# Chunk-selected attention into a soft mixture of experts on one core: the order of five groups of steps

## The chip, the core and the metric
The kernel runs on one core of a Trainium2 chip. The core has a matrix engine (TensorE, PE in the profile, with its weight loads listed as PEld), a vector engine (VectorE, DVE), a scalar engine (ScalarE, ACT), a general engine (GpSimd, POOL) and a queue engine (SyncE, SP). Each takes its own instructions strictly in order; between engines, semaphores make one wait for another. Matrix products are written to PSUM, everything else lies in SBUF. The metric is device time in microseconds (us); every difference below is in us too.

## The reference
Four batches of eight heads, 768 positions, 64 numbers per head. Keys are cut into 24 chunks of 32. Per query, an upper bound of its score with each chunk is worked out from the chunk's smallest and largest key; the six chunks with the highest bounds are kept, and attention runs over those, causally:

```python
k_min = np.min(k_chunks, axis=3)
k_max = np.max(k_chunks, axis=3)
ub = np.sum(np.maximum(q * k_min, q * k_max), axis=-1)      # per query and chunk
ub = np.where(causal, ub, -1e9)
top_chunks = np.argsort(ub, axis=-1)[..., -6:]
scores = np.where(selected & causal_by_position, scale * q @ k.T, -1e9)
x = softmax(scores) @ v                                      # 3072 rows of 512
logits = x @ phi                                             # 32 slots: 8 experts of 4
slot_input = softmax(logits, axis=0).T @ x                   # over all 3072 rows
slot_out = relu(slot_input @ w1[e]) @ w2[e]                  # per expert, 512 -> 1024 -> 512
out = softmax(logits, axis=1) @ slot_out
```

## The kernel before
The heads are worked in 16 pairs, four pairs to a batch. The order of the work is written out by hand: the loop over pairs `i` (from line 618) issues steps of several pairs in turn, and each engine runs its share in just that order. Tiles in PSUM come from three small pools: `sc` (two tiles, scores), `at` (one tile, the attention output) and `tp` (two tiles, everything else: transposes, bounds, logits). A step that takes a tile of `tp` has to wait until the tile two before it has been read.

In turn `i` the steps are, by function and engine:

- `scores(i, g)` for six groups `g`: PE forms scores (L323) and adds a large negative number for chunks not selected (L333); `expo(i, g)`: ACT's exponential into `e_sb` (L347), then POOL zeroes what lies above the diagonal (L357).
- `ubound(i + 1)`: PE's bounds for the next pair, into `ub_ps` (L275, L282), from `qpn` and `bd`.
- `normalise(i - 2)`: DVE's reciprocal and product into `x_sb` (L387, L388), which empties the only `at` tile.
- `select(i + 1)`: DVE finds the largest bounds (`mx`, L294) and marks what falls below the sixth (`ns_t`, L297).
- `transposes(i + 2, "k")`, `evac_T`: PE transposes k into `tr_ps` (L231), ACT copies it to `kT` (L240); the same for q later in the turn.
- `pv(i - 1, ...)`: PE multiplies `e_sb` with v into `at_ps` (L375), in parts spread over the turn; the first part has to find `at` empty.
- `x_transposes(i - 2)`, `evac_x`: PE and DVE transpose `x_sb` (L397, L408).
- `kmin`, `kmax` (i + 2): DVE's smallest and largest keys, `mm` (L249, L255); `kmax` also forms `bd`, one block per head (L257).
- `ns_transposes(i + 1)`, `evac_ns`: PE transposes the marks (L305), DVE copies them to `nsT` (L313), which the next turn's scores need.
- `qsplit(i + 2)`: DVE's negative and positive parts of q, `qpn` (L265, L269).

When the last pair of a batch is through attention, that batch's MoE steps join the turns (`moe(step, i)` acts only on the last pair of a batch). At the end of turns 5, 9 and 13 come the logits (L420) and, on DVE, `pm` and a copy of the logits (L429, L430). Turns 6, 10 and 14 then hold `pmT` (PE, L436), `mb` (DVE, L443), the exponentials of both softmaxes (ACT into `d_sb`, L470, and into `c_pad`, L494 to L498), `moe_dispatch` (PE into `si_ps`, L509; DVE adds to `si_acc`, L516 to L527) and `moe_ct`: PE transposes the combine weights `c_pad` into `cT_ps` (L532) and DVE copies them to `cT_all` (L540).

Behind the loop, the last batch's MoE steps run alone. The experts follow: hidden layer into `h_ps` (L834), ACT's rectification into `h_sb` (L841), transposes into `hT_ps` (L846) and DVE's copy into `hT_pad` (L850), in two halves `f` of the hidden layer. The second layer accumulates in `so_ps`: `experts_out(f)` for experts 0 to 3 (L873), each in a quarter of the rows, `shared_out()` for experts 5 to 7 (L889), whose 24 products are dealt out over the four quarters so that four run beside each other, and `last_expert_out` for expert 4, in two halves of the columns (L899), whose weights are the last to be loaded. `slot_sums` (L854) gives the softmax's sums. `so_part` (L931) and `so_all` (L933, L935) scale the result, and the last products with `cT_all` give the output, which SP's queue writes.

All loads are issued from POOL's queue, in the order in which the steps stand there: q and k five pairs ahead, v two pairs ahead (L162), and the experts' weights one or two to a turn (`load_w`, L145). The weights of the last expert are issued at the start of turn 15.

Of the kernel before, what the change touches and what calls it, by code (L numbers as in the profile page):

```python
# [59 lines left out]
def kernel(  # L60
# [21 lines left out]
    LAST = NPAIR - 1  # L82
# [8 lines left out]
    st = {}  # L91
# [126 lines left out]
    def warm(n):  # L218
        r = ones_sq.rearrange("p (o c) -> p o c", o=1).broadcast_to([P, 4, P])
        for _ in range(n):  # L220
            for x in range(2):
                nc.tensor.matmul(
                    warm_ps[:, 2 * x:2 * x + 2], lhsT=ones_sq, rhs=r[:, :2], start=True, stop=True)

    def transposes(i, nm):

        ps = p_tp.tile([P, NQT, P], BF16, name="tr_ps", tag="tp")
        src = st.pop((nm, i))
        for g in range(NQT):
            for h in range(2):  # L230
                nc.tensor.matmul(  # L231
                    ps[h * 64:(h + 1) * 64, g, :], lhsT=src[:, h, g * D:(g + 1) * D], rhs=ident,
                    is_transpose=True,
                )
        st[nm + "ps", i] = ps

    def evac_T(i, nm):

        t = tp3.tile([P, S], BF16, name=nm + "T", tag=nm + "T")
        nc.scalar.copy(  # L240
            t.rearrange("d (p g) -> d p g", g=NQT),
            st.pop((nm + "ps", i)).rearrange("d g p -> d p g"),
        )
        st[nm + "T", i] = t
# [7 lines left out]
    def kmax(i):  # L252
        kT = st["kT", i].rearrange("d (c x) -> d c x", x=CH)
        mm = st.pop(("mm", i))
        nc.vector.tensor_reduce(mm[:, 1, 0, :], kT, axis=AX.X, op=ALU.max)  # L255
        bd = tpu.tile([P, 2, 2, NCHUNK], BF16, name="bd", tag="bd")
        nc.vector.tensor_tensor(  # L257
            bd, mm.broadcast_to([P, 2, 2, NCHUNK]), headsel.broadcast_to([P, 2, 2, NCHUNK]), op=ALU.mult,
        )
        st["bd", i] = bd  # L260

    def qsplit(i):
        qT = st["qT", i]
        t = tpu.tile([P, 2, S], BF16, name="qpn", tag="qpn")
        nc.vector.tensor_scalar_min(t[:, 0, :], qT, 0.0)  # L265
        if i == 0:
            nc.scalar.activation(t[:, 1, :], qT, func=ACT.Relu)
        else:
            nc.vector.tensor_scalar_max(t[:, 1, :], qT, 0.0)  # L269
        st["qpn", i] = t  # L270
# [40 lines left out]
    def evac_ns(i):  # L311
        t = tp2.tile([P, NJ * P], BF16, name="nsT", tag="nsT")
        nc.vector.tensor_copy(t, st.pop(("nsps", i)).rearrange("p t c -> p (t c)"))  # L313
        st["nsT", i] = t
# [25 lines left out]
    def expo(i, g, masked=True):  # L340
        pieces = (GROUPS_LAST if i == LAST else GROUPS)[g]
        w = sum(x[2] for x in pieces)
        if w == 512:
            e = ep.tile([P, 2, 512], BF16, name="e_sb", tag="e_sb")
        else:
            e = ep3.tile([P, 2, 384], BF16, name="e3_sb", tag="e3_sb")
        nc.scalar.activation(e[:, :, :w], st.pop(("scps", i, g))[:, :, :w], func=ACT.Exp, scale=scale)  # L347

        st["e", i, g] = e
        if masked:  # L350
            mask(i, g)
# [191 lines left out]
    def have(i):  # L543
        return 0 <= i < NPAIR

    def moe(step, i):

        if have(i) and i % NPB == NPB - 1:
            step(i // NPB)
# [5 lines left out]
    def weights(i):  # L555
        nonlocal nw
        for _ in range(wplan.get(i, 0)):
            load_w(nw)
            nw += 1
# [3 lines left out]
    evac_T(0, "k")  # L563
    kmin(0)
    kmax(0)
    warm(2)
    transposes(0, "q")
    evac_T(0, "q")
# [15 lines left out]
    evac_ns(0)  # L584
    kmin(1)
    kmax(1)
    qsplit(1)
    nc.gpsimd.dma_start(out=phi_sb, in_=moe_phi.rearrange("(hg p) s -> p hg s", p=P))
    nc.gpsimd.affine_select(
# [23 lines left out]
    kmin(2)  # L613
    evac_ns(1)
    kmax(2)
    qsplit(2)

    for i in range(1, NPAIR):
        slots = have(i - 3) and (i - 3) % NPB == NPB - 1
        if i >= EARLY:  # L620
            wt = ctx.enter_context(tc.tile_pool(name=f"wt{i}", bufs=1))
            w_sb.append(wt.tile([P, NFG * Dm], BF16, name=f"w_sb{i}"))
            weights(i)
        if have(i + 5) and not slots:
            load(i + 5, "k")
            load(i + 5, "q")
        scores(i, 0)
        expo(i, 0)
        moe(moe_max, i - 3)
        scores(i, 1)  # L630
        expo(i, 1)
        if have(i + 1):
            ubound(i + 1)
        moe(moe_bound, i - 3)
        if have(i - 2):
            normalise(i - 2)
        if i == LAST:
            moe_ct_copy(B - 2)
        if have(i + 1):
            select(i + 1)  # L640
        moe(moe_comb, i - 3)
        if have(i + 2):
            transposes(i + 2, "k")
            evac_T(i + 2, "k")
        if not slots:
            if have(i + 2):
                load_v(i + 2)
            if i < EARLY:
                weights(i)
        pv(i - 1, [0, 1, 2])  # L650
        for g in (2, 3):
            scores(i, g)
            expo(i, g, not slots)
        moe(moe_exp, i - 3)
        if slots:
            mask(i, 2)
            mask(i, 3)
        if have(i + 5) and slots:
            load(i + 5, "k")
            load(i + 5, "q")  # L660
        if have(i - 2):
            x_transposes(i - 2)
        pv(i - 1, [3] if i < LAST else [3, 4])
        if have(i + 2):
            transposes(i + 2, "q")
            evac_T(i + 2, "q")
            kmin(i + 2)
        moe(moe_exp2, i - 3)
        if have(i - 2):
            evac_x(i - 2)  # L670
        if have(i + 2):
            kmax(i + 2)
        moe(moe_scale, i - 3)
        if slots:
            if have(i + 2):
                load_v(i + 2)
            if i < EARLY:
                weights(i)
        scores(i, 4)
        expo(i, 4)  # L680
        if i == LAST:
            pv(i - 1, [5])
        moe(moe_comb2, i - 3)
        scores(i, 5)
        expo(i, 5)
        if have(i + 1):
            ns_transposes(i + 1)
            evac_ns(i + 1)
        if i < LAST:
            pv(i - 1, [4])  # L690
        moe(moe_dispatch, i - 3)
        if i < LAST:
            pv(i - 1, [5])
        if have(i + 2):
            qsplit(i + 2)
        moe(moe_ct, i - 3)
        moe(moe_logits, i - 2)
        moe(moe_copy, i - 2)
        if i == LAST - 2:
            l_ctx.close()  # L700
        if i == LAST - 1:
            u_ctx.close()
# [140 lines left out]
    def hidden_T(f):  # L843
        hT_ps = p_tp.tile([P, 4, P], BF16, name="hT_ps", tag="tp")
        for x in range(4):
            nc.tensor.matmul(hT_ps[:, x, :], lhsT=h_sb[:, f, x::4], rhs=ident, is_transpose=True)  # L846
        for g in range(2):
            o = hT_pad[:, f * 4:(f + 1) * 4, g * 4:(g + 1) * 4, g * SPE:(g + 1) * SPE]
            i_ = hT_ps.rearrange("p a (j s) -> p a j s", j=4)[:, :, :, g * SPE:(g + 1) * SPE]
            nc.vector.tensor_copy(o, i_)  # L850
# [19 lines left out]
    def experts_out(f):  # L870
        for fg in range(f * 4, (f + 1) * 4):
            for e in range(4):
                nc.tensor.matmul(  # L873
                    so_ps[e * CH:(e + 1) * CH, :], lhsT=hT_pad[:, fg, e, :],
                    rhs=w_sb[E + e][:, fg * Dm:(fg + 1) * Dm], start=(fg == 0), stop=False,
                )

    def shared_out():
        parts = [
            [(5, x) for x in range(6)],  # L880
            [(5, 6), (5, 7), (6, 0), (6, 1), (6, 2), (6, 3)],
            [(6, 4), (6, 5), (6, 6), (6, 7), (7, 0), (7, 1)],
            [(7, x) for x in range(2, 8)],
        ]
        for n in range(6):
            for j in range(4):
                e, fg = parts[j][n]
                c0 = e * CH - (SPE if j == e - 5 else 0)
                nc.tensor.matmul(  # L889
                    so_ps[j * CH:(j + 1) * CH, :], lhsT=hT[:, fg, c0:c0 + CH],  # L890
                    rhs=w_sb[E + LATE.index(e)][:, fg * Dm:(fg + 1) * Dm], start=False, stop=(n == 5),
                )
# [31 lines left out]
    w_ctx.close()  # L924
    op = ctx.enter_context(tc.tile_pool(name="op", bufs=5))
    experts_out(0)
    hidden_T(1)
    slot_sums()
    experts_out(1)
    shared_out()  # L930
    nc.vector.tensor_scalar_mul(so_part, so_ps[:, HD:], zinv)  # L931
    last_expert_out(1)
    nc.vector.scalar_tensor_tensor(so_sb[1], so_last, zinv, so_part, op0=ALU.mult, op1=ALU.add)  # L933
# [17 lines left out]
    n = 0  # L951
# [44 lines left out]
```

## Time and profile before

| | |
|---|---|
| median of 3 runs | 161.38 us (161.33 to 162.57) |
| the profiled execution | 161.03 us, span 159.3 us |
| busy PE, DVE, ACT, POOL | 137.7, 122.7, 122.1, 103.0 us |
| chain that ended last, by engine | PE 48%, ACT 17%, DVE 12%, DMA 8% |
| loop over pairs, from the first exponential to the last | about 12.8 to 124.8 us |
| experts' layers | 131.0 to 140.1 us |
| output | 140.1 us to the end |

Busy time is how long an engine had an instruction running. Products on PE overlap each other and their ends are modelled, so a busy PE can still have room. The chain follows the last instruction back, at each step to what released it. In the timelines below, a number in brackets is how long the engine sat idle before the row, and behind the arrow stands what it waited for. "issue" there means that the profile names no other engine.

### The profile page before, as it was taken

Reading aid. Unit: us, or ns where it says so; the run is one execution under the profiler, and the core shown is the slowest. Engines: PE = TensorE matmul, PEld = TensorE weight load, DVE = VectorE, ACT = ScalarE, POOL = GpSimd, SP = SyncE. Lnnn points to the kernel's source line nnn. Section 1 sums busy time; section 2 is a strip of 40 time slices with the busy share of each in tenths; the row PEclk is TensorE's granted clock in tenths of the full one; section 3 lists DMA queues with packets and bytes.
Section 4 is the critical chain, followed back from the end, with each engine's and each line's share of the span. In section 5 each row is a group of like instructions: output and inputs, shape, how many; then the busy total and the mean of one; then the engine's idle time right before and its main releaser. Section 6 shows DMA issues by size and latency. Waiting matters only on the chain.

```text
span 159.3 us, 5926 instructions
## 1 busy us (share of the span) xinstructions
PE 137.7 (86%) x2435; PEld 93.6 (59%) x2436; DVE 122.7 (77%) x436; ACT 122.1 (77%) x168; POOL 103.0 (65%) x201
## 2 busy tenths in 40 slices
PE   7796779999999998999999989999898999978400
PEld 5473446767667776767777766767667854433000
DVE  5367889999999998999999699999952751287620
ACT  3288879999999898999989889998788632076510
POOL 6979779599797679888766976759574710000000
PEclk9999999999999999999999999999999999999965
DMA  2999999999999999999999999999999999239996
GB/s 39 149 179 202 190 208 206 185 203 205 182 208 198 202 207 200 204 183 207 198 203 203 202 203 204 201 207 194 210 203 214 215 214 200 60 116 406 406 402 251
DMA packets 40571, 32.92 MB, mean 207 GB/s; under 512 B 26336, under 2 KB 34784, under 8 KB 40544
## 3 DMA queue, kind: packets, MB, share of 16 engines
q0 software_dynamic: 38384, 26.25, 110.6%
q1 hardware_dynamic: 2160, 6.29, 10.1%
q8 instruction: 19, 0.31, 0.7%
q14 instruction: 8, 0.07, 0.1%
HBM read 52.49 MB, written 6.29 MB: 369 GB/s over the span
## 4 chain that ended last, share of the span: by engine, by line
PE 48%; ACT 17%; DVE 12%; DMA 8%; issue 6%; POOL 4%; DVEq 0%; ACTq 0%; SPq 0%; POOLq 0%
ACT e_sb L347 11%; PE sc_ps L323 9%; PE at_ps L375 8%; PE sc_ps L333 6%; DMA out_dram<-o_sb 5%; PE tr_ps L231 5%; PE xT_ps L397 4%; ACT qT L240 4%; DMA q_in<-in_q_dram 3%; DVE x_sb L388 3%; PE h_ps L834 2%; PE ub_ps L282 2%; PE ub_ps L275 1%; DVE mx L294 1%; PE so_ps L873 1%
## 5 line engine op out<-in xcount | busy, mean ns | idle before, releaser
L347 ACT ACTIVATE e_sb<-sc_ps 128x1024 bf16<-128x1024 f32 (+1 forms) x96 | 83.1, 917 | 6.6 <-PE sc_ps L333 6.0
L357 POOL TENSOR_SCALAR_AFFINE_SELECT e_sb<-e_sb 128x256 bf16<-128x256 bf16 x96 | 39.8, 437 | 12.0 <-ACT e_sb L347 11.6
L323 PE MATMUL sc_ps<-qT,kT 64*128 64x384 bf16 (+3 forms) x258 | 36.8, 306 | 2.6 <-ACT e_sb L347 1.7
L333 PE MATMUL sc_ps<-nsT,smask 64*128 64x384 bf16 (+2 forms) x294 | 38.1, 284 | 0.1
L375 PE MATMUL at_ps<-v_t,e_sb 128*128 128x65 bf16 x642 | 28.4, 194 | 1.6 <-DVE x_sb L388 1.4
L375 PEld LDWEIGHTS <-e_sb 128*128 128x128 bf16 x642 | 24.5, 98 | 3.8 <-issue 2.5
L323 PEld LDWEIGHTS <-kT 64*128 64x128 bf16 x258 | 13.9, 93 | 10.7 <-issue 5.3
L294 DVE MAX8 mx<-ub_ps 128x8 f32<-128x8 f32 (+1 forms) x192 | 16.8, 162 | 4.0 <-PE ub_ps L282 3.8
L162 POOL DMA_DIRECT2D v_t<-in_v_dram x16 | 16.6, 1040 | 3.4 <-PE xT_ps L397 1.4
L249 DVE TENSOR_REDUCE mm<-kT 128x24 bf16<-128x768 bf16 x16 | 15.1, 943 | 3.1 <-ACT kT L240 3.1
L333 PEld LDWEIGHTS <-smask 64*128 64x128 bf16 x294 | 15.0, 94 | 3.8 <-issue 0.6
L240 ACT COPY kT<-tr_ps 128x768 bf16<-128x768 bf16 x16 | 12.9, 804 | 4.3 <-PE tr_ps L231 4.3
L388 DVE TENSOR_TENSOR x_sb<-at_ps,inv 128x768 bf16<-128x768 f32 (+1 forms) x17 | 15.5, 910 | 0.6
L255 DVE TENSOR_REDUCE mm<-kT 128x24 bf16<-128x768 bf16 x16 | 15.1, 943 | 0.0
L240 ACT COPY qT<-tr_ps 128x768 bf16<-128x768 bf16 x16 | 12.8, 799 | 2.8 <-PE tr_ps L231 2.8
L145 POOL DMA_DIRECT2D w_sb<-in_moe_w_dram x16 | 11.4, 714 | 1.5 <-DMA w_sb<-in_moe_w_dram 1.5
L152 POOL DMA_DIRECT2D k_in<-in_k_dram x14 | 10.2, 726 | 3.0 <-PE tr_ps L231 1.6
L152 POOL DMA_DIRECT2D q_in<-in_q_dram x14 | 10.1, 720 | 0.5 <-PE sc_ps L333 0.3
L408 DVE COPY xT_sb<-xT_ps 128x768 bf16<-128x768 bf16 (+1 forms) x15 | 8.0, 537 | 2.5 <-PE xT_ps L397 2.5
L231 PE MATMUL tr_ps<-ident,q_in 128*64 128x128 bf16 x192 | 8.4, 223 | 1.1 <-DMA q_in<-in_q_dram 0.8
L231 PE MATMUL tr_ps<-ident,k_in 128*64 128x128 bf16 x192 | 8.7, 229 | 0.2
L397 PE MATMUL xT_ps<-ident,x_sb 128*128 128x128 bf16 x96 | 8.3, 221 | 0.3 <-DVE x_sb L388 0.3
(147 smaller groups left out, 209.0 us busy)
## 6 DMA issues: line engine op xcount, KB each, us to landing
w_sb<-in_moe_w_dram POOLq DMA_DIRECT2D x16, 1024.0 KB, 15.5
out_dram<-o_sb SPq DMA_DIRECT2D x10, 512.0 KB, 4.6
v_t<-in_v_dram POOLq DMA_DIRECT2D x16, 192.0 KB, 11.6
k_in<-in_k_dram POOLq DMA_DIRECT2D x14, 192.0 KB, 10.6
q_in<-in_q_dram POOLq DMA_DIRECT2D x14, 192.0 KB, 10.9
out_dram<-o_sb SPq DMA_DIRECT2D x2, 256.0 KB, 4.1
k_in<-in_k_dram POOLq DMA_DIRECT2D x1, 384.0 KB, 7.3
q_in<-in_q_dram POOLq DMA_DIRECT2D x1, 384.0 KB, 8.4
```

The costliest lines, as they stand in the source:

```text
L152: nc.gpsimd.dma_start(out=t, in_=src.rearrange("h (p g) d -> p h (g d)", p=P))
L162: nc.gpsimd.dma_start(out=v_t[i % NV][:, :, :, :D], in_=v[b, 2 * j:2 * j + 2].rearrange("h (g p) d -> p h g d", p=P),)
L231: nc.tensor.matmul(ps[h * 64:(h + 1) * 64, g, :], lhsT=src[:, h, g * D:(g + 1) * D], rhs=ident, is_transpose=True,)
L240: nc.scalar.copy(t.rearrange("d (p g) -> d p g", g=NQT), st.pop((nm + "ps", i)).rearrange("d g p -> d p g"),)
L249: nc.vector.tensor_reduce(mm[:, 0, 0, :], kT, axis=AX.X, op=ALU.min)
L294: nc.vector.max(mx[:, a, :], ub[:, a, :max(8, 4 * t + 4)])
L323: nc.tensor.matmul(ps[:, h, c:c + w], lhsT=kT[r, kg * P:(kg + 1) * P], rhs=qT[r, qs], start=True, stop=False,)
L333: nc.tensor.matmul(ps[:, h, c + (f - t0) * P:c + (l - t0) * P], lhsT=smask[r, x, kg].rearrange("p a b -> p (a b)"), rhs=nsT[r, (f - x * NJ ...
L347: nc.scalar.activation(e[:, :, :w], st.pop(("scps", i, g))[:, :, :w], func=ACT.Exp, scale=scale)
L357: nc.gpsimd.affine_select(out=e[:, :, c:c + P], in_=e[:, :, c:c + P], compare_op=ALU.is_ge, fill=0.0, base=0, pattern=[[0, 2], [1, P]], ch ...
L375: nc.tensor.matmul(o, lhsT=st["e", i, g][:, h, c:c + P], rhs=v_t[i % NV][:, h, kg, :], start=(kg == 0), stop=(kg == t),)
L388: nc.vector.tensor_tensor(st["x", b][:, t0:t1, 2 * j:2 * j + 2, :].rearrange("p t h d -> p h t d"), at[:, :, :, :D], inv.broadcast_to([P, ...
```

## The change
Five things are moved; the instructions and their number stay the same on every engine.

1. In the loop, the transposes of k for pair i + 2, with ACT's copy, stand ahead of the bounds of pair i + 1, instead of behind the selection. On PE that puts twelve transposes ahead of thirteen products. ACT's and POOL's own orders stay as they were.
2. `bd` is taken out of `kmax` into `by_head`, and in the loop stands behind `evac_ns`: DVE copies the marks to `nsT` before it forms `bd`.
3. For batches 0 and 1, `moe_ct` (PE's transposes of the combine weights and DVE's copy) comes at the end of turns 7 and 11 instead of 6 and 10. For batch 2 it stays at the end of turn 14.
4. The 24 products of the shared experts are dealt out anew, so that the first twelve need only the first half of the hidden layer.
5. They are issued in three parts: four products ahead of the second half's transposes, eight behind these, and twelve behind `experts_out(1)`.

Because of the first and third, tiles of `tp` are taken in another order too: in an ordinary turn the tile two before the transposes of x is now that of k's transposes, read by ACT, and no longer that of the bounds, read by DVE.

```diff
         nc.vector.tensor_reduce(mm[:, 1, 0, :], kT, axis=AX.X, op=ALU.max)
+        st["mm", i] = mm
+
+    def by_head(i):
+        mm = st.pop(("mm", i))
         bd = tpu.tile([P, 2, 2, NCHUNK], BF16, name="bd", tag="bd")
...
         scores(i, 1)
         expo(i, 1)
+        if have(i + 2):
+            transposes(i + 2, "k")
+            evac_T(i + 2, "k")
         if have(i + 1):
             ubound(i + 1)
...
         moe(moe_comb, i - 3)
-        if have(i + 2):
-            transposes(i + 2, "k")
-            evac_T(i + 2, "k")
...
         if have(i + 1):
             ns_transposes(i + 1)
             evac_ns(i + 1)
+        if have(i + 2):
+            by_head(i + 2)
...
-        moe(moe_ct, i - 3)
+        if i < LAST - 1:
+            moe(moe_ct, i - 4)
+        elif i == LAST - 1:
+            moe(moe_ct, i - 3)
...
-    def shared_out():
+    def shared_out(ns):
         parts = [
-            [(5, x) for x in range(6)],
-            [(5, 6), (5, 7), (6, 0), (6, 1), (6, 2), (6, 3)],
-            [(6, 4), (6, 5), (6, 6), (6, 7), (7, 0), (7, 1)],
-            [(7, x) for x in range(2, 8)],
+            [(5, x) for x in (0, 1, 2, 4, 5, 6)],
+            [(5, 3), (6, 0), (6, 1), (5, 7), (6, 4), (6, 5)],
+            [(6, 2), (6, 3), (7, 0), (6, 6), (6, 7), (7, 4)],
+            [(7, x) for x in (1, 2, 3, 5, 6, 7)],
         ]
-        for n in range(6):
+        for n in ns:
...
     experts_out(0)
+    shared_out((0,))
     hidden_T(1)
+    shared_out((1, 2))
     slot_sums()
     experts_out(1)
-    shared_out()
+    shared_out((3, 4, 5))
```
Ahead of the loop, `by_head` is called right behind each `kmax`, so nothing changes there.

More of the change, by code (lines that the diff above doesn't have):

```diff
@@ L565 @@
     kmax(0)
+    by_head(0)
     warm(2)
@@ L586 @@
     kmax(1)
+    by_head(1)
     qsplit(1)
@@ L615 @@
     kmax(2)
+    by_head(2)
     qsplit(2)
```

## The prediction
> **What bounds the kernel now.** I read the page's GB/s line first, then the stretches cut at the start of `ub_ps` of successive pairs, the list of waits, and the timeline inside one pair. The page (GB/s in 40 slices of 3.98 us) and three stretches (length, then busy us of PE, PEld, DVE, ACT, POOL):
> ```profile
> GB/s 39 149 179 202 190 208 206 185 203 205 182 208 198 202 207 200 204 183 207 198 203 203 202 203 204 201 207 194 210 203 214 215 214 200 60 116 406 406 402 251
> ...
> 34.66:41.17 6.51, 6.42 (x130) 4.52 (x126) 6.22 (x23) 6.48 (x9) 6.39 (x13) 1.00 1.24 201
> 54.78:62.67 7.89, 7.75 (x163) 5.82 (x159) 7.43 (x28) 7.09 (x13) 6.46 (x13) 1.00 1.35 202
> 69.62:76.12 6.50, 6.41 (x129) 4.51 (x126) 6.40 (x23) 6.46 (x9) 5.93 (x12) 1.00 1.53 198
> ```
> An ordinary pair takes 6.51 us; ACT works 6.48 of it, PE 6.42, DVE 6.22 to 6.40. ACT has no slack, PE and DVE next to none, so an ordinary pair can't get shorter by reordering; a pair that carries MoE steps (the middle row) takes 1.38 longer. There order matters. The waits (us, times, longest) say who is late:
> ```profile
> ACT e_sb L347 <- PE sc_ps L333: 6.0, 11, 0.8
> DVE mx L294 <- PE ub_ps L282: 3.8, 8, 1.6
> PE at_ps L375 <- DVE x_sb L388: 1.4, 3, 0.6
> ```
> ACT waits for PE's scores, PE sometimes for DVE's `x_sb`, DVE for PE's bounds. One ordinary pair in order of time (start, length):
> ```profile
> 33.92 0.96 DVE L388 TENSOR_TENSOR x_sb<-at_ps,inv 128x768 bf16<-128x768 f32 x1
> 34.89 0.53 PE L231 MATMUL tr_ps<-ident,k_in 128*64 128x128 bf16 x12
> 35.07 1.05 DVE L294 MAX8 mx<-ub_ps 128x8 f32<-128x8 f32 x12 [0.19 <-PE ub_ps L282]
> 35.35 0.55 PE L375 MATMUL at_ps<-v_t,e_sb 128*128 128x65 bf16 x12
> 35.60 0.81 ACT L240 COPY kT<-tr_ps 128x768 bf16<-128x768 bf16 x1
> ...
> 38.78 0.86 PE L375 MATMUL at_ps<-v_t,e_sb 128*128 128x65 bf16 x22
> 39.20 0.35 DVE L313 COPY nsT<-ns_ps 128x384 bf16<-128x384 bf16 x1
> 39.62 0.39 PE L323 MATMUL sc_ps<-qT,kT 64*128 64x512 bf16 x2
> 40.27 1.94 ACT L347 ACTIVATE e_sb<-sc_ps 128x1024 bf16<-128x1024 f32 x2
> ```
> ACT's copy of k starts without a wait. `scores` of the next pair follow the last `pv` at once and the first exponential 0.65 us later: what is put on PE there reaches ACT in full.
>
> **k ahead of bounds, pairs 1 to 13.** Nothing is added; twelve transposes, 0.46 us (34.89 to 35.35), go in front of `ub_ps`. In an ordinary pair ACT gains nothing, since k wasn't late. DVE's `mx` starts 0.46 later; beside its 0.19 wait DVE idles 6.51 - 6.22 - 0.19 = 0.10, so it falls about 0.36 behind PE and stays there. What takes that: `x_sb` ends at 34.88 + 0.46 = 35.34, and `pv` waits for it at 35.35. That is a tie; cover 0.01.
>
> In pair 1, PE stands still in front of the second half of the bounds:
> ```profile
> 20.64 0.87 DVE L269 TENSOR_SCALAR qpn<-qT 128x768 bf16<-128x768 bf16 x1
> 21.57 0.45 PE L282 MATMUL ub_ps<-bd,qpn 128*128 128x48 bf16 x11 [0.59 <-DVE qpn L269]
> 21.95 0.53 PE L231 MATMUL tr_ps<-ident,k_in 128*64 128x128 bf16 x12
> 22.52 0.80 ACT L240 COPY kT<-tr_ps 128x768 bf16<-128x768 bf16 x1 [0.72 <-PE tr_ps L231]
> ```
> The transposes fit into that wait, ACT's copy loses its 0.72, the bounds end as before: PE and ACT gain up to 0.46, I take **-0.40**, while DVE's own times stay. From here to the first MoE pair the ordering costs nothing, since DVE's lag is just this lead.
>
> **Where the lag is paid.** Logits of a finished batch come at the end of pairs 5, 9 and 13; `pm` must follow DVE's queue, and PE's `pmT`, the second scores and, through `x_sb`, `pv` follow `pm`:
> ```profile
> 52.70 0.57 DVE L269 TENSOR_SCALAR qpn<-qT 128x768 bf16<-128x768 bf16 x1
> 53.29 0.36 DVE L429 TENSOR_REDUCE pm<-lg_ps 128x32 f32<-128x192 f32 x1
> ...
> 113.96 1.51 ACT L347 ACTIVATE e_sb<-sc_ps 128x768 bf16<-128x768 f32 x2 [0.81 <-PE sc_ps L333]
> ```
> `qpn` ends at 53.27 and `pm` starts at 53.29: no cover. So each of the three MoE pairs gives 0.36 of lag to ACT; at the third ACT waits for PE already (0.81). The bounds per MoE pair are 0 and 0.46. Sum **+0.36 x 3 = +1.08**; the first of them uses up pair 1's lead.
>
> **Combine transposes, batches 0 and 1.** PE's `cT_ps` and DVE's copy leave the end of pairs 6 and 10 for the end of 7 and 11; batch 2's stay:
> ```profile
> 60.95 0.51 PE L532 MATMUL cT_ps<-ident,c_pad 128*128 128x128 bf16 x6
> 61.39 0.39 PE L323 MATMUL sc_ps<-qT,kT 64*128 64x512 bf16 x2
> 62.04 1.94 ACT L347 ACTIVATE e_sb<-sc_ps 128x1024 bf16<-128x1024 f32 x2 [0.45 <-PE sc_ps L333]
> 62.09 0.54 DVE L540 COPY cT_all<-cT_ps 128x768 bf16<-128x768 bf16 x1
> 63.81 0.54 PE L375 MATMUL at_ps<-v_t,e_sb 128*128 128x65 bf16 x12 [0.39 <-DVE x_sb L388]
> ```
> Removed: PE's 0.44 and ACT's wait of 0.45, and 62.09 to 62.55, 0.46 of DVE, from ahead of the `x_sb` that `pv` waits for: **-0.46** each; late next is that `x_sb`. Added in pairs 7 and 11: the same 0.44 of PE between `pv` and `scores`, where ACT has no slack (40.27 above): **+0.44** each, bounds 0.2 (if PE arrives early) and 0.46; the copy's 0.46 on DVE lies beside that delay. Two moves: -0.04.
>
> **The copy of the selection.** All sixteen `bd` (shortest, median, longest in ns):
> ```profile
> L257 DVE TENSOR_TENSOR bd<-mm,headsel x16: 257/334/478, 8.3 to 109.2; 128x96 bf16<-128x96 bf16 x16
> ```
> `bd` goes behind `nsT`. With PE 0.40 ahead, the scores start at 39.62 - 0.40 = 39.22 and their mask products soon after; `nsT` would end at 39.55, and without `bd` ahead of it between 39.07 and 39.29. That makes it no gain, but keeps the lead of pair 1 from being lost here, 0.3 if the cover were gone. `bd` itself is needed only by the next pair's bounds. No DMA and nothing on POOL's queue or SP's is moved.
>
> **Shared experts.** The chain (start, us, what) in the tail, then the first product of the last expert, and the last weight load's issue and landing:
> ```profile
> 135.11 0.86 PE so_ps L873 x16
> 135.97 0.35 PE hT_ps L846 x4
> 136.32 0.31 PE z_ps L854 x2
> 136.63 1.02 PE so_ps L873 x16
> 137.65 1.32 PE so_ps L889 x24
> ...
> 139.60 0.49 DVE so_all L933
> ...
> 138.94 0.40 PE L899 MATMUL so_last<-w_sb,hT_pad 128*32 128x256 bf16 x8
> 138.94 0.20 PEld L899 LDWEIGHTS <-hT_pad 128*32 128x32 bf16 x8 [0.29 <-issue]
> ...
> L145 POOL DMA_DIRECT2D w_sb<-in_moe_w_dram x1: 765/765/765, 117.9 to 117.9; - x1
> ...
> DMA to landing us min/median/max: 21.0/21.0/21.0
> ```
> Half of the 24 products (0.055 each) now stand around the transposes, so the copy to `hT_pad`, which PE now waits for between `z_ps` and its next products, hides behind eight of them. I count `z_ps` itself as 0.10, an estimate between 0 and its 0.31. From 135.11: 16 products 0.86, four 0.22, transposes 0.35, eight 0.44, `z_ps` 0.10, 16 products 0.86, twelve 0.66: 3.49, against 137.65 + 1.32 - 135.11 = 3.86: **-0.37** (bounds 0, and 0.47 if all waits in `z_ps` and in the 1.02 go).
>
> The sixteen products behind `z_ps` took 1.02, the like sixteen at 135.11 took 0.86: a change from full-width to quarter-width products costs 0.16 at most here, and twice more of it would leave 0.05 of the 0.37. The Trainium skill (TensorEngine Tiling (Array Packing), Key Properties) says that changing the tiling mode drains the TensorE; that speaks against the interleaving, which adds two such changes, and the two rows agree that something is lost there.
>
> There is a floor. The last weights land at 117.92 + 21.0 = 138.92, and the first `so_last` runs at 138.94, its weights having been held back for 0.29 with no engine named: the load it was. The GB/s line is flat at about 200 through the loop: the loads are a stream with a backlog, and compute that finishes early doesn't bring its end forward. Below it there is only `so_part` starting sooner: `so_last` is done at 138.94 + 0.40 = 139.34 against 139.60 now: at most -0.2.
>
> **Sum:** -0.40 + 1.08 - 0.04 - 0.37 = +0.27, with about 0.05 for ties: **+0.3**. The profiled execution took 161.03 (span 159.3), so 161.3; it lay 0.35 under the median of 161.38, to which I add the same: **161.7**.
>
> **Rivals.**
> - *No lag.* DVE absorbs the 0.36 at the MoE pairs: without 1.08 the sum is -0.8, and the landing holds it at -0.2: 161.2. For it: the flat stream. Against it: `pm` has no cover. If the landing itself can move, 160.6.
> - *DVE's ring binds* (the slower one). `x_sb`, `pv`, next pair's `ub_ps`, `mx`, next `x_sb` form a ring over two pairs: PE from `pv` to the next bounds' end 6.51 - 0.46 = 6.05; hand-over 0.18 (34.89 to 35.07); DVE from `mx` to the next `x_sb`'s end 34.88 + 6.51 - 35.07 = 6.32; in all 12.55 of 13.02. With k in front it is 13.01: no slack. From there each DVE microsecond counts half in every pair. `bd` ranges over 0.22 and `qpn` over 0.30 (0.57 and 0.87 above); 0.3 more in a pair would be 0.15 over 12 pairs: +1.8, less 0.37: 162.8. The Trainium skill (SBUF — State Buffer, SBUF: two separate sides) has VectorE and GpSimd share a port pair by an exclusive lock; `bd` is now later, among POOL's masks. By that rule such growth is likelier; the spread of `bd` agrees that something holds it up at times.
> - *The tail gives nothing*, through changes of shape: +0.7, 162.1.
>
> **How the numbers follow.** Forecast 0.42, no lag 0.28 (0.05 of it with a landing that moves), ring 0.13, tail 0.17. A measurement of this kernel tells about 1%, 1.6 us, from no change. Faster by over that needs the landing to move further than any case: 0.06. Slower by over that is the ring's upper half, 2.4 in place of 1.8: 0.09. The range goes from 160.7 (no lag, early landing) to 162.7 (just under the ring's middle).
>
> **What would show it.** Right: in pair 1 `kT` starts at about 22; `mx` starts some 0.4 later relative to `x_sb`'s pair; `pm` stands behind `qpn`, not behind `lg_ps`; ACT's 0.45 at 62.04 is gone and a wait of about 0.4 appears at the first exponential of pairs 8 and 12; `so_ps` ends about 3.5 after it starts. Wrong: `x_sb` waits listed in ordinary pairs (ring); or the last load landing well off 138.9, which would take the floor away.

## The result and the profile after

The changed kernel took 162.52 us (median of 19 runs, 161.71 to 163.45), the kernel before 161.13 beside it (19 runs): a ratio of **1.0085, 95% interval 1.0064 to 1.0106**, some 1.4 us slower. The profiled execution took 162.11 with a span of 160.4, 1.1 over the span before.

Where it went is read from stretches cut at one recurring event, the start of the first 768-wide exponential of a pair. First the kernel before (from, to, length; then busy us of PE, PEld, DVE, ACT, POOL with instruction counts, granted clock, DMA share, GB/s): pairs 5 to 14 as a whole, then the stretches that end in pairs 6, 10 and 14.

```profile
49.45:113.96 64.51, 62.31 (x1231) 45.08 (x1227) 61.27 (x220) 59.54 (x80) 50.71 (x100) 1.00 1.36 201
49.45:56.58 7.13, 7.13 (x151) 5.17 (x147) 6.87 (x26) 6.47 (x8) 4.50 (x11) 1.00 1.39 203
77.89:85.03 7.14, 7.14 (x151) 5.17 (x147) 6.92 (x26) 6.47 (x8) 4.37 (x9) 1.00 1.37 202
106.83:113.96 7.13, 6.70 (x139) 4.78 (x135) 6.88 (x26) 5.78 (x7) 5.79 (x11) 1.00 1.31 202
```

The same stretches of the changed kernel, with the one from pair 2 to pair 3 added, and two lines of its list of waits; the line behind the mark is of the kernel before:

```profile
49.43:114.99 65.56, 62.18 (x1231) 44.85 (x1227) 60.95 (x221) 59.39 (x80) 51.34 (x101) 1.00 1.37 201
29.27:36.38 7.11, 6.42 (x126) 4.52 (x122) 7.01 (x26) 6.50 (x9) 6.80 (x14) 1.00 1.60 198
49.43:56.99 7.56, 7.26 (x151) 5.26 (x147) 7.19 (x26) 6.58 (x8) 5.05 (x11) 1.00 1.36 201
78.21:85.72 7.51, 7.24 (x151) 5.17 (x147) 7.14 (x28) 6.62 (x9) 4.66 (x9) 1.00 1.36 202
107.44:114.99 7.55, 6.81 (x139) 4.81 (x135) 7.33 (x29) 5.93 (x8) 6.04 (x12) 1.00 1.35 200
```
```profile
ACT e_sb L351 <- PE sc_ps L337: 8.2, 19, 0.9
PEld pmT_ps L440 <- DVE pm L433: 1.7, 3, 0.6
...
PEld pmT_ps L436 <- DVE pm L429: 0.6, 3, 0.2
```

Three things are to be seen. Both kernels reach pair 5 at the same time (49.45 and 49.43): the changed kernel is 0.56 ahead at pair 1 (22.87 in place of 23.43), and this lead is gone by then. Pairs 6, 10 and 14 are longer by 0.43, 0.37 and 0.42, together 1.22, where the whole of pairs 5 to 14 is longer by 1.05. And a wait has grown: the weight load for `pmT` waits for DVE's `pm` three times, once for each finished batch, as it did before, but 1.7 in all in place of 0.6.

The end of turn 9 in the changed kernel shows that wait:

```profile
81.48 0.59 DVE L269 TENSOR_SCALAR qpn<-qT 128x768 bf16<-128x768 bf16 x1
81.99 0.56 DVE L273 TENSOR_SCALAR qpn<-qT 128x768 bf16<-128x768 bf16 x1
82.47 0.34 DVE L433 TENSOR_REDUCE pm<-lg_ps 128x32 f32<-128x192 f32 x1
82.87 0.28 PE L440 MATMUL pmT_ps<-identf,pm 128*32 128x128 f32 x1 [0.27 <-DVE pm L433]
```

`pm` stands right behind `qpn`, and PE idles 0.27 for it; in the kernel before this product (at 82.18) follows without such a wait. The lead of the first pairs goes in pair 2's turn, on DVE and POOL, and ACT then waits:

```profile
31.71 0.34 PE L309 MATMUL ns_ps<-ident,ns_t 128*128 128x128 bf16 x3 [0.17 <-POOL ns_t L300]
32.54 1.07 DVE L269 TENSOR_SCALAR qpn<-qT 128x768 bf16<-128x768 bf16 x1
32.61 1.73 POOL L361 TENSOR_SCALAR_AFFINE_SELECT e_sb<-e_sb 128x256 bf16<-128x256 bf16 x4
35.32 0.54 PE L379 MATMUL at_ps<-v_t,e_sb 128*128 128x65 bf16 x12 [0.53 <-PE ub_ps L286]
36.38 1.51 ACT L351 ACTIVATE e_sb<-sc_ps 128x768 bf16<-128x768 f32 x2 [0.41 <-PE sc_ps L337]
```
The same instruction in the same turn of the kernel before:
```profile
32.90 0.34 DVE L265 TENSOR_SCALAR qpn<-qT 128x768 bf16<-128x768 bf16 x1
```

The first half of `qpn` took 1.07 in place of 0.34, while POOL's four masks ran beside it. PE's wait in front of `at_ps` is put down to `ub_ps`, PE's own work, which was long done; what came last there is `x_sb`, which DVE started at 34.26 and ended at 35.22, after that `qpn`. Ahead of that, PE waited 0.17 for POOL's `ns_t` (a cast that forms one column of the marks, L296 in the kernel before; the list of steps leaves it out), and ACT's first exponential of pair 3 waited 0.20 for the scores behind it. These 0.20 and 0.41 are the 0.61 by which the stretch to pair 3 is longer than before (7.11 in place of 6.50).

In the tail the chain (start, us) is no shorter than before, 136.15 to 140.08 (3.93) against 135.11 to 138.97 (3.86):

```profile
136.15 0.86 PE so_ps L885 x16
137.01 0.22 PE so_ps L901 x4
137.22 0.35 PE hT_ps L858 x4
137.57 0.55 PE so_ps L901 x8
138.12 0.31 PE z_ps L866 x2
138.42 0.98 PE so_ps L885 x16
139.40 0.68 PE so_ps L901 x12
```
```profile
L145 POOL DMA_DIRECT2D w_sb<-in_moe_w_dram x1: 767/767/767, 119.0 to 119.0; - x1
DMA to landing us min/median/max: 19.4/19.4/19.4
```

The last weights landed at 119.0 + 19.4 = 138.4, ahead of their first use.

### The profile page after: what moved, and what is told of

It is laid out like the page before. It is cut to its first block, busy times and chain, and to the rows that moved or that the text cites. A ratio compares the mean times of both kernels' runs of the same rounds, so it can differ in the third digit from the quotient of the medians.

```text
span 160.4 us, 5938 instructions
## 1 busy us (share of the span) xinstructions
PE 136.6 (85%) x2435; PEld 92.9 (58%) x2436; DVE 121.9 (76%) x436; ACT 121.8 (76%) x168; POOL 103.2 (64%) x201
## 4 chain that ended last, share of the span: by engine, by line
PE 34%; DVE 17%; DMA 16%; ACT 14%; POOL 10%; issue 6%; DVEq 0%; POOLq 0%; SPq 0%; ACTq 0%
DMA q_in<-in_q_dram 10%; ACT e_sb L351 8%; PE sc_ps L327 5%; DMA out_dram<-o_sb 5%; DVE mx L298 5%; PE at_ps L379 4%; PE tr_ps L231 4%; PE sc_ps L337 4%; PE xT_ps L401 3%; ACT qT L240 3%; POOL e_sb L361 3%; PE h_ps L846 2%; PE ub_ps L286 2%; DVE ns_t L301 2%; DVE mm L255 2%
## 5 line engine op out<-in xcount | busy, mean ns | idle before, releaser
L231 PEld LDWEIGHTS <-k_in 128*64 128x64 bf16 x192 | 5.8, 109 | 5.2 <-issue 4.1
```

The source lines that it names most:

```text
L231: nc.tensor.matmul(ps[h * 64:(h + 1) * 64, g, :], lhsT=src[:, h, g * D:(g + 1) * D], rhs=ident, is_transpose=True,)
```

## The experiments

The theories that the expectations name: **L**, the recorded one, that k ahead of the bounds makes DVE late and that this is paid at `pm` in pairs 6, 10 and 14; **M**, that the moved combine transposes, and **T**, that the tail, carry the difference. Each kernel was run beside the kernel before on the same chip. This table gathers what the profiles gave: the stretches defined above as differences to the kernel before, summed where several pairs stand together, and the turns in which one `qpn` instruction took over 1 us. Each row is of one profiled execution; those of e7, e8, e11 and e12 were the slowest executions of their kernels. "To 5" is from pair 1 to pair 5, so it begins behind the place where k ahead gains its lead, and the loss of that lead stands there as a plus; counted from pair 0, the changed kernel has -0.03.

| | ratio, 95% interval | to 5 | 6 | 7 to 9 | 10 | 11 to 13 | 14 | 5 to 14 | `qpn` over 1 us |
|---|---|---|---|---|---|---|---|---|---|
| changed kernel | 1.0085 (1.0064 to 1.0106) | +0.54 | +0.43 | -0.09 | +0.37 | -0.08 | +0.42 | +1.05 | turn 2 |
| e1 k ahead alone | 1.0131 (1.0097 to 1.0165) | +1.13 | +1.13 | +0.47 | 0 | +0.35 | +0.86 | +2.81 | 5, 13 |
| e2 combine transposes alone | 0.9986 (0.9957 to 1.0015) | +1.31 | 0 | -0.21 | -0.01 | -0.21 | 0 | -0.43 | none |
| e3 shared experts alone | 0.9982 (0.9955 to 1.001) | +0.46 | 0 | +0.02 | -0.01 | 0 | 0 | +0.01 | 3 |
| e4 copy alone | 1.009 (1.0055 to 1.0124) | +0.84 | 0 | 0 | +0.06 | 0 | +0.76 | +0.82 | 1, 4, 13 |
| e5 all but the copy | 1.0151 (1.0099 to 1.0204) | +1.47 | +1.05 | +0.28 | +0.07 | +0.17 | +0.93 | +2.50 | 5, 13 |
| e6 copy, masks late | 1.0196 (1.0135 to 1.0257) | +4.56 | 0 | +0.01 | 0 | +0.28 | -0.18 | +0.11 | none |
| e7 changed, masks late | 1.0322 (1.0268 to 1.0375) | +6.82 | +1.04 | -0.18 | +0.05 | +0.19 | -0.17 | +0.93 | 3 |
| e8 k late in 5, 9, 13 | 1.0122 (1.0076 to 1.0168) | +1.16 | 0 | +0.10 | +0.07 | +0.02 | +0.76 | +0.95 | 1, 4, 13 |
| e9 e2 and e3 together | 0.9983 (0.9957 to 1.0009) | +0.52 | 0 | -0.20 | -0.01 | -0.20 | 0 | -0.41 | 3 |
| e10 e9, k ahead in turn 1 | 1.0003 (0.9978 to 1.0028) | +0.95 | 0 | -0.20 | -0.01 | +0.26 | 0 | +0.05 | none |
| e11 e9, `z_ps` sooner | 0.9981 (0.9953 to 1.001) | +1.45 | 0 | -0.20 | -0.01 | -0.21 | +0.01 | -0.41 | none |
| e12 changed, masks late in 2, 9, 13 | 1.0072 (1.0046 to 1.0098) | +0.24 | +1.41 | +0.04 | +0.04 | -0.09 | +0.04 | +1.44 | 1, 5 |

The opening up to pair 5 can't be used for comparisons: e2, e3, e9 and e11 have the same instructions there as the kernel before and differ from it by 0.46 to 1.45. In e2 and e11 nearly all of it is one wait, in e3 and e9 about half: ahead of pair 3, PE waits for POOL's cast `ns_t`, which stands behind POOL's load of k (1.43 and 1.57 in e2 and e11, where that load was held for 2.43 and 2.42; 0.34 and 0.40 in e3 and e9, held for 1.38 and 1.35). The stretches behind it repeat to 0.02 where nothing is changed (the row of e3), with one exception in e10.

### The four parts one by one

**e1**, k ahead of the bounds alone:
```diff
         expo(i, 1)
+        if have(i + 2):
+            transposes(i + 2, "k")
+            evac_T(i + 2, "k")
         if have(i + 1):
             ubound(i + 1)
...
         moe(moe_comb, i - 3)
-        if have(i + 2):
-            transposes(i + 2, "k")
-            evac_T(i + 2, "k")
```


> The kernel before with only k's transposes ahead of the bounds. Theory L (the lag): PE gains about 0.5 us in pair 1, loses it again to DVE by pair 3 to 6, and each of the three MoE pairs then pays 0.4 to 0.6 us because pm and x_sb stand behind a later mx; sum +1.0 us (ratio about 1.006). Rival M (the moved combine transposes are what costs): pair 1's gain stays, the sum is -0.4 to 0 us. Rival T (the tail): 0 us.

Measured 1.0131: the sign is L's, the place too but for pair 10, the size is twice it. The end of turn 13 in e1 says why (DVE and POOL):
```profile
111.77 1.62 POOL L357 TENSOR_SCALAR_AFFINE_SELECT e_sb<-e_sb 128x256 bf16<-128x256 bf16 x4
111.94 1.20 DVE L265 TENSOR_SCALAR qpn<-qT 128x768 bf16<-128x768 bf16 x1
113.53 0.34 DVE L429 TENSOR_REDUCE pm<-lg_ps 128x32 f32<-128x192 f32 x1
```
The masks start just ahead of `qpn`, `qpn` takes 1.20, and `pm` behind it is late by that as well. In pair 10, whose `qpn` took 0.35 and 0.56 (0.56 and 0.55 before), e1 loses nothing: 0.36 isn't paid by rule in each of the three.

**e2**, the combine transposes of batches 0 and 1 one pair later, alone:
```diff
-        moe(moe_ct, i - 3)
+        if i < LAST - 1:
+            moe(moe_ct, i - 4)
+        elif i == LAST - 1:
+            moe(moe_ct, i - 3)
```


> The kernel before with only the combine transposes of batches 0 and 1 one pair later. Theory L: the 0.45 us saved in pairs 6 and 10 and the 0.46 us paid at the end of pairs 7 and 11 cancel, 0 us within 0.2. Rival M: +0.8 to +1.0 us, since an ordinary pair has no slack and the saved time is covered by DVE anyway.

No difference by the ratio; in the stretches a gain of 0.4 in pairs 7 and 11 and a loss of 0.2 in the pairs behind them. M falls.

**e3**, the shared experts alone (dealt out anew as in the change; those lines are left out here):
```diff
     experts_out(0)
+    shared_out((0,))
     hidden_T(1)
+    shared_out((1, 2))
     slot_sums()
     experts_out(1)
-    shared_out()
+    shared_out((3, 4, 5))
```


> The kernel before with only the shared experts' products dealt anew and issued in three parts. Theory of changes of array shape: nothing is gained, -0.05 to +0.1 us, so_ps runs from its first to its last product in 3.9 us as before. The prediction's step: -0.2 to -0.37 us. Rival T: +0.3 us or more, out of the output that follows.

No difference by the ratio, and a chain from `so_ps` to the last shared product of 3.94 (3.86 before). T falls too.

**e4**, `bd` behind the copy of the marks, alone:
```diff
         if have(i + 1):
             ns_transposes(i + 1)
             evac_ns(i + 1)
+        if have(i + 2):
+            by_head(i + 2)
...
         nc.vector.tensor_reduce(mm[:, 1, 0, :], kT, axis=AX.X, op=ALU.max)
+        st["mm", i] = mm
+
+    def by_head(i):
+        mm = st.pop(("mm", i))
         bd = tpu.tile([P, 2, 2, NCHUNK], BF16, name="bd", tag="bd")
```


> The kernel before with only bd behind the copy of the selection's marks. Theory L: 0 us within 0.2, no wait hangs on it while PE isn't early. Rival (port): bd and the next steps on DVE fall among POOL's masks and grow, and DVE being near its limit costs 0.1 us a pair, +0.5 us or more.

Measured 1.009: L's nothing was wrong. The port rival was right that the steps fall among the masks and grow, but the cost is not 0.1 in each pair: it falls in three turns. DVE and POOL at the end of turn 1:
```profile
25.74 0.36 DVE L317 COPY nsT<-ns_ps 128x384 bf16<-128x384 bf16 x1 [0.41 <-PE ns_ps L309]
25.95 1.54 POOL L361 TENSOR_SCALAR_AFFINE_SELECT e_sb<-e_sb 128x256 bf16<-128x256 bf16 x4
26.01 0.48 DVE L261 TENSOR_TENSOR bd<-mm,headsel 128x96 bf16<-128x96 bf16 x1
26.42 1.28 DVE L269 TENSOR_SCALAR qpn<-qT 128x768 bf16<-128x768 bf16 x1
```
`bd` used to fill DVE's wait for `ns_ps`. Now DVE idles 0.41 there, `bd` comes behind it, and `qpn` starts after the masks have begun. It then takes 1.28 and ends at 27.70, just behind the masks (25.95 + 1.54 = 27.49), which run at 0.385 apiece. The three turns with such a `qpn` are the ones that lose: +0.41 and +0.43 within the opening, +0.76 in pair 14.

### What goes together, and the masks moved out of the way

**e5**, the changed kernel with `bd` back in `kmax`, ahead of `nsT` (the edit of e4 undone; the three other parts as in the change):
```diff
-        if have(i + 2):
-            by_head(i + 2)
```


> The changed kernel with bd back in front of nsT (so: k ahead, combine transposes later, shared experts dealt anew). Theory S (each part's cost stands by itself, the copy's 0.9% included): the changed kernel's 1.0085 less 0.009, ratio 0.999 to 1.001. Theory I (the copy costs when it is alone, but with k ahead it repairs something, since nsT then is what the scores wait for): 1.3% of k ahead alone less 0.3% of the two other parts, ratio 1.009 to 1.012, and ACT waits of 0.5 or more at the first exponentials of pairs 2 and 3 as with k ahead alone.

1.0151 lies clear of S. Theory I's ratio (1.009 to 1.012) lies below the measured one, though partly inside its interval; the waits it named are there (0.56 and 1.10), but PE waits in front of them for POOL's `ns_t` (0.70 and 1.07), which stands on POOL and not behind `bd`. The copy costs 0.9% alone; beside k ahead the kernel with it is 0.7% faster, with intervals that just overlap. In both cases what the stretches show is whether `qpn` falls on the masks (turns 5 and 13 here).

**e6**, e4 with the masks of groups 2 to 4 started later:
```diff
+    BY_LOAD = (1, 2, 3, 4, 7, 8)
...
             load(i + 5, "k")
+            late_masks()
             load(i + 5, "q")
...
             qsplit(i + 2)
+        if waiting and i not in BY_LOAD:
+            junk = tpu.tile([P, 12], BF16, name="junk", tag="junk")
+            nc.gpsimd.tensor_copy(junk, st["qpn", i + 2][:, 1, :12])
+            late_masks()
```


> Only the copy sooner, as before (1.009), and with it GpSimd's four masks at a turn's end put behind the next turn's first load (turns 1 to 4, 7, 8) or behind DVE's second qpn (5, 9, 11 to 13), so that they start when DVE has finished qpn. Theory P (the copy's price is that DVE's qpn, standing later, falls on the masks and takes 1.28 in place of 0.35): no qpn over 0.7, ratio 1.000 to 1.004. Rival W (the price is nsT's wait for ns_ps, which bd no longer fills): the long qpn go, but the ratio stays at 1.007 to 1.010. Both agree that masks too late for pv would show as PE waiting for POOL.

**e7**, the same edit on the changed kernel.

> The changed kernel with the same four masks started later. Theory P: qpn of pair 2's turn takes 0.35 in place of 1.07, so the lead of 0.5 of pairs 1 and 2 lives on, and DVE has 0.2 to 0.4 more room in every pair: ratio 1.000 to 1.004. Rival L (the lag of DVE is paid at pm whatever qpn takes): lead kept but paid away in pairs 6, 10 and 14, ratio 1.005 to 1.008.

Both ratios missed, through a fault of the experiment. In e6, the whole of pairs 5 to 14, then pairs 1 to 2 and 2 to 3, and the load that the masks stood behind:
```profile
53.34:117.96 64.62, 62.41 (x1231) 45.02 (x1227) 59.45 (x220) 59.53 (x80) 50.23 (x104) 1.00 1.35 200
22.76:33.06 10.30, 6.93 (x118) 4.51 (x116) 6.60 (x23) 6.47 (x9) 7.42 (x15) 0.91 1.42 197
33.06:40.33 7.27, 7.18 (x126) 4.97 (x122) 5.12 (x21) 6.57 (x9) 5.46 (x12) 0.90 1.25 206
```
```profile
29.62 0.71 POOL L152 DMA_DIRECT2D k_in<-in_k_dram  x1 [2.86 <-DMA w_sb<-in_moe_w_dram]
```
POOL sat 2.86 in front of that load for an earlier transfer of weights, and the masks, and so `pv`, with it: 3.8 us in one pair. In the kernel before, the masks stand ahead of the load; what such a wait can make late there is the cast `ns_t` behind it, as in e2 and e11. Behind the opening e6 answers its question: with no long `qpn`, pairs 5 to 14 take 64.62 against 64.51 before, where e4 took 65.33. The copy's price there is the collision. e7's pairs 10 and 14 (+0.05 and -0.17) point the same way; its +1.04 in pair 6, where PE's scores at 62.80 waited 0.93, is not explained.

**e8**, the changed kernel, k at its old place in turns 5, 9 and 13:
```diff
-        if have(i + 2):
+        if have(i + 2) and i not in (5, 9, 13):
             transposes(i + 2, "k")
             evac_T(i + 2, "k")
...
         moe(moe_comb, i - 3)
+        if have(i + 2) and i in (5, 9, 13):
+            transposes(i + 2, "k")
+            evac_T(i + 2, "k")
```


> The changed kernel with k's transposes at their old place in turns 5, 9 and 13 alone, the turns that end with the logits and pm. Theory L (k ahead makes DVE late by 0.36, and pm hands this to PE and ACT in three pairs): pm comes 0.3 to 0.5 sooner against the exponentials, ratio 1.0085 - 1.1/161 = 1.002. Rival P (the time is lost where qpn falls on GpSimd's masks, wherever that is): 1.006 to 1.010.

The ratio speaks for P (1.0122), the stretches for L and P at once:
```profile
80.54:87.75 7.21, 7.21 (x151) 5.14 (x147) 6.70 (x25) 6.48 (x9) 4.35 (x9) 1.00 1.28 205
109.57:117.46 7.89, 6.77 (x139) 4.78 (x135) 7.53 (x26) 5.89 (x7) 5.55 (x11) 1.00 1.42 202
```
Pairs 6 and 10 are back at 7.13 and 7.21, as L expected. Only pair 10 tells L from P: its two `qpn` took 1.11 together (1.15 in the changed kernel), while those of pair 6 took 0.91 in place of 1.19. Pair 14 is longer than in the changed kernel, since its `qpn` at 112.73 now takes 1.28, and e4's other collisions, in turns 1 and 4, are back as well.

**e12**, the changed kernel with the masks behind DVE's second `qpn` in turns 2, 9 and 13 and no load in between:
```diff
+    LATER = (2, 9, 13)
...
             qsplit(i + 2)
+        if i in LATER:
+            junk = tpu.tile([P, 12], BF16, name="junk", tag="junk")
+            nc.gpsimd.tensor_copy(junk, st["qpn", i + 2][:, 1, :12])
+            for g in (2, 4, 3):
+                mask(i, g)
```


> The changed kernel, its four masks at a turn's end started only behind DVE's second qpn in turns 2, 9 and 13, with no load moved. Theory D (DVE's queue ahead of x_sb and pm counts in full, whether it is late by k's 0.46 or by masks that stretch qpn): qpn 0.35 and 0.35 in these turns, the steps at pairs 3 (+0.61), 10 (+0.37) and 14 (+0.42) shrink to 0.1 or less, pair 6's +0.43 stays; ratio 1.000 to 1.003. Rival O (the pace is PE's order: with k ahead the bounds are 0.46 later whatever DVE takes): the qpn shrink but pairs 10 and 14 keep 0.3 or more, ratio 1.005 to 1.008.

DVE at the end of turn 9, and the stretches to pairs 3, 10, 14 and 6:
```profile
82.94 0.35 DVE L269 TENSOR_SCALAR qpn<-qT 128x768 bf16<-128x768 bf16 x1
83.21 0.35 DVE L273 TENSOR_SCALAR qpn<-qT 128x768 bf16<-128x768 bf16 x1
83.56 0.36 DVE L433 TENSOR_REDUCE pm<-lg_ps 128x32 f32<-128x192 f32 x1
...
53.14 1.53 DVE L269 TENSOR_SCALAR qpn<-qT 128x768 bf16<-128x768 bf16 x1
```
```profile
30.25:36.66 6.41, 6.32 (x126) 4.46 (x122) 5.53 (x21) 6.41 (x9) 5.33 (x12) 1.00 1.56 201
49.78:58.32 8.54, 7.24 (x151) 5.18 (x147) 8.14 (x27) 6.61 (x10) 4.76 (x11) 1.00 1.33 202
79.67:86.85 7.18, 7.18 (x151) 5.18 (x147) 6.79 (x28) 6.51 (x9) 4.41 (x10) 1.00 1.34 204
108.56:115.73 7.17, 6.74 (x139) 4.81 (x135) 6.93 (x29) 5.82 (x8) 5.85 (x13) 1.00 1.34 201
```
With k still ahead in all turns, pairs 10 and 14 fall from 7.51 and 7.55 to 7.18 and 7.17 (7.14 and 7.13 before), and pair 3 from 7.11 to 6.41. So theory D holds in the three turns that were shielded, and O falls: what is paid at `pm` is DVE's lateness, 0.4 of it from k's place, and 0.4 less time in `qpn` (0.70 for both halves in place of 1.15) pays it off. The ratio missed nevertheless (1.0072, not 1.000 to 1.003): in turn 5, not shielded, `qpn` met the masks for 1.53, and pair 6 took 8.54. In the profiled execution that one event ate what the three turns had given. A kernel with all such turns shielded was not run.

### A version that beats both?

**e9**, the edits of e2 and e3 together (k and the copy as in the kernel before).

> The two parts that cost nothing when alone, together: combine transposes of batches 0 and 1 later, shared experts dealt anew; k and the copy of the selection as in the kernel before. Additive: 0.9986 x 0.9982 = 0.997, between 0.994 and 1.000, pairs 5 to 14 at 64.1 us (64.51 before). If the combine transposes' 0.4 is given back behind the loop, where the last weights are waited for: 0.999 to 1.001 with a shorter loop.

0.9983, interval 0.9957 to 1.0009: faster than the changed kernel, not to be told from the kernel before. Pairs 5 to 14 gain their 0.41, and then the first product of the last expert waits for its weights:
```profile
138.46 0.40 PE L902 MATMUL so_last<-w_sb,hT_pad 128*32 128x256 bf16 x8 [0.21 <-DMA w_sb<-in_moe_w_dram]
```

**e10**, e9 with k's transposes ahead of the bounds in turn 1 alone:
```diff
+        if have(i + 2) and i == 1:
+            transposes(i + 2, "k")
+            evac_T(i + 2, "k")
         if have(i + 1):
             ubound(i + 1)
...
-        if have(i + 2):
+        if have(i + 2) and i > 1:
```


> e9_ct_shared with k's transposes ahead of the bounds in turn 1 alone. If pair 1's lead can live (the recorded forecast's -0.40, with no lag afterwards since k is at its old place): 0.4 below e9_ct_shared, ratio 0.993 to 0.996. If DVE holds the pace there (its nsT and x_sb come no sooner, so the scores of pairs 2 and 3 wait for it): the lead is gone by pair 4, ratio as e9_ct_shared, and ACT waits appear at the first exponentials of pairs 2 and 3.

The lead dies, by pair 3. Counted from pair 0, pair 1's first 768-wide exponential comes 0.55 sooner than in e9, that of pair 3 0.12 later. ACT's first exponentials of pairs 2 and 3 wait 0.39 and 0.80 for scores, as the second explanation expected. But they don't wait for DVE. The wait ahead of pair 3:
```profile
31.59 0.25 POOL L296 CAST ns_t<-mx 128x12 bf16<-128x12 f32 x1
31.89 0.34 PE L305 MATMUL ns_ps<-ident,ns_t 128*128 128x128 bf16 x3 [0.77 <-POOL ns_t L296]
32.27 0.36 DVE L313 COPY nsT<-ns_ps 128x384 bf16<-128x384 bf16 x1 [0.53 <-PE ns_ps L305]
...
33.52 1.94 ACT L347 ACTIVATE e_sb<-sc_ps 128x1024 bf16<-128x1024 f32 x2 [0.80 <-PE sc_ps L333]
```
DVE's `mx` had ended at 28.57, and DVE sat idle for PE; PE waited for POOL's cast, which stood behind POOL's loads of k and q and two masks. The load of k had been held for 1.34. In turn 1 it is the same (PE waits 0.53 for the cast), and in e1 (0.69 and 0.76). This is read off the waits; no run moved the cast. The +0.26 in pairs 11 to 13 can't come from the edit, which lies in turn 1: in turn 10 the second `qpn` took 0.72 (0.34 in e9), PE waited 0.45 for it, and pair 11 took 0.47 longer than in e9.

**e11**, e9 with `slot_sums()` ahead of the second part of the shared experts:
```diff
     hidden_T(1)
-    shared_out((1, 2))
     slot_sums()
+    shared_out((1, 2))
```


> e9_ct_shared with z_ps directly behind the transposes of the hidden layer, ahead of the eight shared products. If the tail is lost in changes of shape (four products 0.22 but eight of them 0.55 behind the transposes, sixteen 0.98 behind z_ps, 0.86 elsewhere): one change fewer, the chain from the first so_ps to the last shared product 0.1 to 0.25 shorter than in e9_ct_shared, ratio 0.001 lower at most. If z_ps's 0.31 is its own length, not a wait for its place: nothing.

0.9981 (0.9953 to 1.001). In PE's timeline, whose stretches begin up to 0.2 ahead of the chain's, the time from the first `so_ps` to the end of the last shared product is 3.96 in place of 4.07 in e9: 0.11 less, the low end of what one change of shape was to give; the `z_ps` step stays 0.31 long at its new place (136.76 to 137.07), so that is its own length. By 138.37 + 0.82 = 139.19 PE was done, and waited for the weights until 139.75: the gain can't be seen in the time.

## Why the prediction was right or wrong

It gave 161.7 with a range of 160.7 to 162.7 and "within 1%" as the likeliest. The measured 162.52 is inside, near the upper end, and nearer to two of the rivals (162.1 and 162.8) than to the forecast; the rise was +1.4 in place of +0.3. Term by term:

- **The lag paid at `pm`, +0.36 x 3 = +1.08**: right in place, mechanism and size (+0.43, +0.37 and +0.42). The rival "no lag" falls. It needs one addition: it is paid because DVE also spends 0.45 there in `qpn` stretched by POOL's masks (0.59 and 0.56 in place of 0.35 each). e8 takes the lag away in pairs 6 and 10, e12 the stretch in pairs 10 and 14, and in pair 10, where each leaves the other in place, either alone brings the pair back. That the size came out in all three pairs is in part luck: the `qpn` of the changed kernel are only 0.04 to 0.13 longer there than before, while the same lag cost 1.13, 0 and 0.86 in e1, as `qpn` fell on the masks or not.
- **The lead of pair 1, -0.40**: it came (0.56 at pair 1; 0.55 in e10 beside e9) and did not last. The step that failed is "From here to the first MoE pair the ordering costs nothing, since DVE's lag is just this lead". Nothing on POOL's queue was moved, and the step left POOL out: its cast `ns_t` comes no sooner, because it stands behind loads that are held, and PE's transposes of the marks wait for it (e10: 0.53 and 0.77). In the changed kernel 0.20 of the lead goes that way and 0.41 through `qpn`'s 1.07, so that `pv` waits for `x_sb`. The copy was to keep the lead, and didn't. In e12, shielded in turn 2, 0.32 of the lead is still there at pair 5, counted from pair 0 (one profile, in an opening that varies). The wait of 0.72 was one execution's: in e9, with the same instructions, ACT's copy waits 0.20, since `qpn` took 0.35 and not 0.87, and yet the lead in e10 is 0.55:
```profile
21.65 0.80 ACT L240 COPY kT<-tr_ps 128x768 bf16<-128x768 bf16 x1 [0.20 <-PE tr_ps L231]
```
- **The combine transposes, -0.04**: right as a sum (about -0.02 a move in the changed kernel, -0.21 in e2), the two sides smaller than taken: -0.15 and +0.13 for -0.46 and +0.44. ACT's 0.45 at 62.04 is gone, as foretold, and the wait at the first exponential of pair 8 is there with 0.29:
```profile
69.28 1.94 ACT L351 ACTIVATE e_sb<-sc_ps 128x1024 bf16<-128x1024 f32 x2 [0.29 <-PE sc_ps L337]
```
- **The copy of the selection, nothing**: wrong by itself (+0.9%), and perhaps a gain beside k ahead (e5 against the change, where the intervals just overlap). The step looked for a cover at the scores and left out what a wait of DVE for `ns_ps` does behind it: it moves `qpn` against POOL.
- **The shared experts, -0.37**: nothing came. `z_ps` was counted as 0.10, the low side of its bounds, and takes 0.31; the eight products take 0.55, not 0.44, and the sixteen 0.98, not 0.86. The three together are 0.44. The prediction had priced this itself (up to 0.16 for a change of shape, twice more of it leaving 0.05) and kept it for a rival, out of the sum. The rule cited from the Trainium skill (TensorEngine Tiling (Array Packing), Key Properties), that a change of tiling mode drains the TensorE, agrees: each change of shape costs 0.11 to 0.12 here, and e11, with one fewer, gets 0.11 back. The rival "the tail gives nothing" was right in this term.
- **The floor**, the last landing at 138.92: it moves with the issue on POOL (117.2 in e9, 119.0 in the changed kernel), did not bind in the changed kernel, and binds in e9 and e11.
- **The slower rival, DVE's ring**: it didn't bind in ordinary pairs (6.41 in the one to pair 4). The rule beside it (SBUF — State Buffer, "SBUF: two separate sides", of the Trainium skill: VectorE and GpSimd share a port pair by an exclusive lock) is what the long `qpn` look like: 0.35 alone, 1.07 to 1.69 beside POOL's masks. The same section lets whichever starts first keep the pair; the rows at 32.54 and 53.14 have `qpn` first, by 0.07 and 0.18, and long all the same (starts on POOL are rough, so this is not settled). It works in single turns, not in each, and through `qpn`, not `bd`.

Summed on the two profiles, which differ by 1.1: the lead lost (0.4) and the tail (0.4) account for the 0.8 between +0.3 and +1.1; the 0.14 that the lag took beyond its 1.08 comes back in the pairs between. The medians differ by 0.3 more than the profiles, and nothing here says where.

## What to carry to other kernels

Giving one engine a lead is worth little when another one sets the pace of the next stage: ask first whose clock the next stage keeps, and look at every engine that has a hand in it (here a small cast on POOL, behind loads). A step whose duration spreads (here `qpn`, 0.34 to 0.87 in the profile of before) is to be priced by what runs beside it and by what the change moves it against, and not by its usual value; an edit that merely delays it by 0.3 can cost 0.8. And compare profiles where unchanged code repeats: here the opening differed by up to 1.45 between kernels with the same instructions, the pairs behind it mostly by 0.02, and once by 0.47.

## What the runs showed of the hardware

- DVE's bf16 `qpn` of 768 columns takes 0.35 alone. In some turns in which POOL's masks had begun 0.03 to 0.66 ahead of it, it took 1.20 to 1.69, the length of several masks (0.385 each), not of one; begun 0.07 or 0.18 ahead of them it still took 1.07 (at 32.54) or 1.53 (e12 at 53.14; masks from 53.32). In other turns the two alternate, with starts just as close (0.56 in the kernel before at 80.82, masks from 80.74): then `qpn` takes 0.35 to 0.65 and four masks 1.6 to 1.9 in place of 1.49 (e12 at 34.08). The starts alone don't tell which will happen.
- The 0.87 of `qpn` at 20.64 in the kernel before had no mask beside it. In the four profiles that show it (before, changed, e4, e12) it began 0.38 to 0.50 behind the start of POOL's issue of a `v_t` load and ended 0.16 behind its end; in the others, at 0.35, it began ahead of that start, at most 0.07 behind it, or clear of that issue. Issues of weights ran beside a `qpn` of 0.34 in many turns, so this is not a rule.
- After PE had stood still in e6 (6.93 busy of 10.30), the granted clock was 0.91 in that stretch and 0.90 in the next, where 126 products took 7.18, against 6.42 at 1.00 (the changed kernel's stretch to pair 3). That stretch was 7.27 long in place of 6.50: the stall seems to have gone on costing in the pair behind it, though nothing isolates the clock.
- A load on POOL's queue sat 2.86 us behind an earlier transfer of weights (e6), and all that stood behind it on POOL waited too.
